# A new order of steps for a linear-attention and feed-forward kernel, with six weight casts on GpSimd

## The chip, the cores and the metric

The kernel runs on one core of one Trainium2 chip. The metric is the device time of one execution in microseconds, as the median of several runs. Three runs of the kernel before took 241.68, 242.40 and 242.57 us, a median of 242.4.

## The reference

Eight batches with eight heads, 576 rows and 64 columns go through a linear attention; its result, seen as 4608 tokens of 512, goes through a feed-forward block.

```python
def phi(x):
    return np.where(x > 0, x, np.exp(x) - 1.0) + 1.0
q_p, k_p = phi(q), phi(k)
kv = np.einsum('bhsd,bhse->bhde', k_p, v)
z = np.sum(k_p, axis=2)
num = np.einsum('bhsd,bhde->bhse', q_p, kv)
den = np.einsum('bhsd,bhd->bhs', q_p, z)[..., None] + 1e-06
x = (num / den).transpose(0, 2, 1, 3).reshape(4608, 512)
h = (x @ w1) * (x @ w2) @ w3        # w1, w2: 512 x 1024, w3: 1024 x 1024
out = h @ w_out                     # w_out: 1024 x 512
```

All inputs and the output are float32 in HBM.

## The kernel before

The kernel is one long list of steps. Every step has a short name, and `ORDER` at the top of the file is the list of these names in the order in which their instructions are issued; each engine works through its own instructions in that order. A letter at the end of a name picks the engine of the step's copy or cast (a ScalarE, v VectorE, p GpSimd), or the queue of a store.

The parts of the work and their steps:

- **Loads.** `L3.i` and `LH.i.x` load blocks of w3 (a block of 128 rows, or half of its columns), `LO.x` a slice of 256 rows of w_out, `LA.x` and `LB.x` pieces of w1 and w2, `LK.b.h`, `LQ.b.h` and `LV.b.h` four heads (half h) of a batch b of k, q and v. All are issued on SyncE's queue. They share 13 buffers, which are handed on in the order in which they come free. A weight piece is 512 KB, a half of a batch 576 KB.
- **w3 @ w_out, computed once.** `C3.i` casts a w3 block to bf16 (blocks without that step stay fp32), `CO.x` casts a w_out slice (line 217), `T3.i.x` transposes half x of a block on TensorE against an identity (four products, line 251) and copies it out of PSUM (line 252), `FW.i.x` multiplies two of the block's eight columns with the w_out slice x (two products, line 263); `FW.i.3` also casts the finished block out (line 265). `CA` and `CB` cast the pieces of w1 and w2 (lines 221 and 226).
- **Attention.** `EX` (ScalarE), `PT` and `PM` (VectorE) make phi of a half of k or q; `VC` casts v. `KV.b.h` or `KB.b` forms k_p^T v with a column of ones for z. `QP.b.h` transposes phi(q) on TensorE (nine products), `QD.b.h` by a DMA. `ND.t` makes numerator and denominator of 128 tokens and divides; `NT.t` does the products and reciprocals of three such tiles, `NM.t.i` their divisions. `XP.t` transposes a tile of x on TensorE, `XD.c.m` two tiles by a DMA.
- **Feed-forward.** Tokens are taken in nine chunks of 512. `F.c.f` is one of eight column blocks f of chunk c: four products with w1 (a), four with w2 (b), a copy of a on ScalarE, and the product a*b on VectorE. For the first chunk f 0 to 3 are split: `FI.0.f.side` is one side, `FP.0.f.side.g` one side for half of the tokens. `O.t` multiplies a tile with w3 @ w_out (eight products) and copies it out; `S.t` stores it with two DMAs, and `Q.35` is the last tile, in pieces.
- **Start.** `I.0` clears a zero tile on VectorE, `I.1` builds the fp32 identity and its bf16 copy on GpSimd, `I.2` sets the ones beside v. `H.n.i` issues n fp32 products of zeros on TensorE whose result nobody reads; there are five in all (three in `H.3.0`), and the profile counts each as two.

PSUM is handed out as four tiles for products of 512 columns (`mm`) and two larger ones (`at`), again in the order in which they come free; `T3`, `QP`, `KV` and `ND` take `at`.

The cast of a w_out slice, and the step that builds the identity, read:

```python
    def s_CO(x, e):
        copy_of(e)(out=wo_sb[:, 2 * x:2 * x + 2].rearrange("p c n -> p (c n)"), in_=raw["wo", x])
        give("ld", ("wo", x))
    ...
        elif i == 1:
            make_identity(nc, ident32)
            nc.gpsimd.tensor_copy(out=ident, in_=ident32)
```

Of the kernel before, what the change touches and what calls it, by code (L numbers as in the profile page):

```python
# [18 lines left out]


ORDER = """
I.0 H.3.0 L3.2 LO.0 I.1 T3.2.0.a H.1.1 CO.0.v FW.2.0.a T3.2.1.a H.1.2 LO.1 CO.1.a L3.4 T3.4.0.v
T3.4.1.v L3.3 T3.3.0.a LO.2 FW.4.0.v FW.4.1.a LO.3 L3.5 T3.3.1.v C3.5.a CO.2.v FW.2.1.a FW.2.2.a
CO.3.v FW.2.3.v L3.6 C3.6.v FW.3.0.a FW.3.1.v LK.0.0 T3.5.0.v LH.0.0 T3.5.1.v LQ.0.0 FW.4.2.v
EX.k.0.0 PT.k.0.0 FW.4.3.a EX.q.0.0 T3.6.0.v PM.k.0.0 FW.5.0.v FW.5.1.v L3.1 T3.6.1.a PT.q.0.0
PM.q.0.0 L3.7 FW.5.2.v FW.6.0.a FW.3.2.a FW.3.3.v FW.5.3.v LQ.0.1 T3.1.0.a C3.7.v T3.1.1.a FW.1.0.v
FW.1.1.a LK.0.1 PT.q.0.1 EX.q.0.1 PM.q.0.1 T3.7.0.a FW.6.1.v FW.6.2.a FW.6.3.a LV.0.0 I.2 T3.0.0.v
LV.0.1 EX.k.0.1 PT.k.0.1 T3.7.1.a LH.0.1 FW.7.0.a FW.7.1.v FW.1.2.v VC.0.0.v QP.0.0.v QP.0.1.a
FW.7.2.a KV.0.0.a PM.k.0.1 VC.0.1.v FW.7.3.v FW.1.3.a KV.0.1.v T3.0.1.a ND.0 FW.0.0.v LA.6 ND.1
FW.0.1.v CA.6.a LA.7 CA.7.a ND.2 FW.0.2.a XP.0.a XP.1.a ND.3 FW.0.3.a FP.0.0.0.0 LB.6 LQ.1.1  # L30
EX.q.1.1 LB.7 LA.3 XP.2.v XP.3.v FP.0.1.0.0 CB.7.a LA.2 FP.0.1.0.1 LB.3 PT.q.1.1 PM.q.1.1 FI.0.2.0
FI.0.3.0 CB.6.v FI.0.1.1 LB.2 CA.2.a LQ.1.0 CB.3.v FP.0.0.0.1 FI.0.0.1 FI.0.3.1 CB.2.v QP.1.1.v
CA.3.a PT.q.1.0 LK.1.0 FI.0.2.1 PT.k.1.0 EX.q.1.0 PM.q.1.0 F.0.4 EX.k.1.0 PM.k.1.0 F.0.5 LV.1.0
VC.1.0.a F.0.6 LK.1.1 EX.k.1.1 PT.k.1.1 PM.k.1.1 LV.1.1 LK.3.0 KV.1.0.a VC.1.1.a F.0.7 LQ.3.1
QP.1.0.a KV.1.1.v PT.k.3.0 EX.q.3.1 EX.k.3.0 O.0.a LQ.3.0 EX.q.3.0 PT.q.3.1 ND.4 ND.5 O.1.a XP.4.a
ND.6 ND.7 PM.k.3.0 LK.2.0 XP.5.a O.2.a PM.q.3.1 XP.6.v XP.7.v LQ.2.1 EX.k.2.0 LQ.2.0 PT.k.2.0
PM.k.2.0 PT.q.3.0 EX.q.2.0 LK.3.1 PM.q.3.0 O.3.a LV.4.1 F.1.0 LV.2.0 LK.4.1 S.0.s F.1.1 PT.q.2.1
EX.q.2.1 S.1.s PT.k.3.1 F.1.2 EX.k.3.1 PM.k.3.1 LK.2.1 PM.q.2.1 F.1.3 VC.2.0.a LV.2.1 PT.k.2.1
PT.q.2.0 PM.q.2.0 EX.k.2.1 F.1.4 LV.3.0 F.1.5 VC.2.1.a PM.k.2.1 F.1.6 LV.3.1 VC.3.0.v QD.2.1
EX.k.4.1 KB.2.a QD.2.0 VC.3.1.a ND.8 QD.3.0 F.1.7 KB.3.a NT.9 NM.9.0 NM.9.1 QD.3.1 XD.2.0 NM.9.2  # L40
XD.2.1 S.2.s LK.4.0 O.4.v O.5.v NT.12 LV.4.0 NM.12.0 O.6.v NM.12.1 O.7.v NM.12.2 LQ.4.1 PT.k.4.0
F.2.0 F.2.1 F.2.2 F.2.3 F.2.4 EX.k.4.0 PT.k.4.1 LQ.5.1 F.2.5 PM.k.4.1 F.2.6 VC.4.0.a LQ.4.0 VC.4.1.a
PM.k.4.0 F.2.7 S.3.s S.4.s LQ.5.0 LK.5.1 PT.q.5.0 EX.q.5.0 NT.15 PM.q.5.0 EX.q.4.1 NM.15.0 PT.q.4.1
PM.q.4.1 PT.q.4.0 LQ.7.1 S.5.s KB.4.a PT.k.5.1 O.8.v EX.k.5.1 S.6.s LK.5.0 EX.k.5.0 PT.k.5.0 XD.3.0
XD.3.1 O.9.a O.10.a O.11.v LV.5.1 F.3.0 PM.k.5.1 LK.6.0 F.3.1 PM.k.5.0 EX.q.4.0 NM.15.1 NM.15.2
LV.5.0 S.7.s S.8.s LK.6.1 F.3.2 S.9.s S.10.s VC.5.0.v PM.q.4.0 QD.4.0 EX.k.6.0 QD.4.1 F.3.3 F.3.4
EX.q.5.1 PT.q.5.1 PM.q.5.1 PT.k.6.1 F.3.5 F.3.6 F.3.7 QD.5.1 O.12.v NT.18 QD.5.0 NM.18.0 XD.4.0
NM.18.1 VC.5.1.a PT.k.6.0 KB.5.a XD.4.1 LQ.6.1 O.13.a O.14.v PT.q.7.1 O.15.v F.4.0 EX.q.7.1 PM.q.7.1
F.4.1 F.4.2 NM.18.2 LK.7.0 F.4.3 NT.21 EX.k.6.1 NM.21.0 NM.21.1 NM.21.2 LV.6.0 VC.6.0.v F.4.4 F.4.5
S.11.s S.12.s PT.k.7.0 LK.7.1 LQ.7.0 F.4.6 LV.6.1 VC.6.1.v S.13.s S.14.s F.4.7 PT.q.7.0 PM.k.6.1  # L50
LQ.6.0 PM.k.6.0 O.16.v EX.q.7.0 O.17.v PM.q.7.0 PT.q.6.1 LV.7.0 O.18.v XD.5.0 XD.5.1 EX.q.6.1
PM.q.6.1 LV.7.1 VC.7.0.a S.15.s EX.q.6.0 KB.6.a NT.24 O.19.v NM.24.0 PT.q.6.0 PM.q.6.0 QD.6.1 F.5.0
VC.7.1.v EX.k.7.1 PT.k.7.1 F.5.1 F.5.2 EX.k.7.0 NM.24.1 NM.24.2 QD.7.1 PM.k.7.0 F.5.3 F.5.4 QD.6.0
PM.k.7.1 F.5.5 S.16.s S.17.s NT.27 XD.6.0 NM.27.0 NM.27.1 QD.7.0 KB.7.a NM.27.2 F.5.6 XD.6.1 XD.7.0
F.5.7 S.18.s NT.30 S.19.s O.20.v S.20.s F.6.0 NM.30.0 NM.30.1 NM.30.2 F.6.1 XD.7.1 O.21.v NT.33
O.22.v NM.33.0 NM.33.1 O.23.v F.6.2 F.6.3 F.6.4 F.6.5 F.6.6 F.6.7 F.7.0 F.7.1 F.7.2 F.7.3 F.7.4
F.7.5 F.7.6 S.21.s S.22.s S.23.s XD.8.0 NM.33.2 XD.8.1 O.24.a O.25.v O.26.v O.27.v S.24.s S.25.s
S.26.s S.27.s F.7.7 F.8.0 F.8.1 F.8.2 F.8.3 F.8.4 F.8.5 F.8.6 F.8.7 O.28.a O.29.a O.30.a S.28.s
S.29.s S.30.s O.31.v S.31.s O.32.v S.32.s O.33.v S.33.s O.34.a S.34.b Q.35
"""  # L60


# [540 lines left out]
```

## Time and profile before

| | |
|---|---|
| median of three runs | 242.4 us |
| the profiled execution | 241.85 us |
| its span, first to last instruction | 240.1 us |
| TensorE busy | 230.6 us (96%) |
| VectorE busy | 158.2 us (66%) |
| ScalarE busy | 113.9 us (47%) |
| GpSimd busy | 1.3 us (1%) |
| moved by DMA | 55.79 MB |

PE is TensorE's products, PEld its weight loads, DVE VectorE, ACT ScalarE, POOL GpSimd, SP SyncE. A row of busy time by stretches gives the stretch, its length, then busy time and count of instructions of PE, PEld, DVE, ACT and POOL, the granted clock of TensorE, the share of the DMA engines and GB/s. A row of the timeline gives start, duration, engine, line, operation, what it writes and reads, shapes and a count where several are merged; in brackets stands the idle time ahead of it and what ended that. A row of the chain of waits gives start, duration, what it was. Products of TensorE are pipelined: the ends are modelled, and the last of a group shows its full latency.

### The profile page before, as it was taken

To read this page: it belongs to the slowest core of one execution; us is meant where nothing else is said; L and a number is where in the kernel's file an instruction comes from. 1 tells how busy PE (TensorE), PEld (TensorE's weight loads), DVE (VectorE), ACT (ScalarE), POOL (GpSimd) and SP (SyncE) were. 2 spreads that over 40 slices of the span, in tenths; PEclk is the share of its full clock that TensorE was granted. 3 is DMA by queue.
4 is the path that set the end of the run, shared out by engine and by line. 5 is a ranking of instruction groups with operands and counts; after the bars stand their busy time and mean duration, and the time that the engine had idled before them with its cause. 6 is when DMAs were issued, how large, how long until landed. Compare 5 with 4: busy or idle time off the path is not lost.

```text
span 240.1 us, 5470 instructions
## 1 busy us (share of the span) xinstructions
PE 230.6 (96%) x2227; PEld 115.8 (48%) x2246; DVE 158.2 (66%) x287; ACT 113.9 (47%) x166; POOL 1.3 (1%) x9
## 2 busy tenths in 40 slices
...
GB/s 245 418 376 405 387 387 390 388 391 389 397 272 155 183 362 360 319 195 317 257 111 279 381 369 211 123 202 111 137 120 83 3 0 44 163 15 0 45 155 149
DMA packets 52040, 55.79 MB, mean 232 GB/s; under 512 B 31280, under 2 KB 31536, under 8 KB 52016
## 3 DMA queue, kind: packets, MB, share of 16 engines
...
q8 instruction: 17, 0.28, 0.5%
...
## 4 chain that ended last, share of the span: by engine, by line
PE 90%; DMA 5%; DVE 1%; issue 1%; SPq 1%; ACT 0%
PE a_ps L482 26%; PE b_ps L482 26%; PE o_ps L535 24%; PE wf_ps L263 6%; DMA w<-in_moe_w_dram 3%; PE nd L398 2%; DMA qt<-phq 2%; PE w3p L251 2%; PE kbp L340 1%; PE qp L368 1%; PE xp L457 1%; PE kvp L340 1%; DVE w3t L252 1%; SPq L157 1%; DVE xt L458 0%
## 5 line engine op out<-in xcount | busy, mean ns | idle before, releaser
L482 PEld LDWEIGHTS <-w_sb 128*128 128x128 bf16 x584 | 56.4, 98 | 66.9 <-issue 0.9
L491 ACT COPY a_sb<-a_ps 128x512 f32<-128x512 f32 x72 | 42.1, 585 | 80.9 <-PE a_ps L482 79.0
L493 DVE TENSOR_TENSOR ab<-a_sb,b_ps 128x512 bf16<-128x512 f32 x72 | 49.1, 686 | 39.3 <-PE b_ps L482 37.5
L482 PE MATMUL a_ps<-xt,w_sb 128*128 128x512 bf16 (+1 forms) x296 | 74.0, 374 | 0.1
L482 PE MATMUL b_ps<-xt,w_sb 128*128 128x512 bf16 x288 | 73.8, 380 | 0.0
L535 PE MATMUL o_ps<-wf_sb,ab 128*128 128x512 bf16 (+2 forms) x290 | 63.5, 368 | 1.2 <-issue 0.6
L535 PEld LDWEIGHTS <-ab 128*128 128x128 bf16 x304 | 28.3, 98 | 31.2
L542 DVE COPY o_sb<-o_ps 128x512 f32<-128x512 f32 x23 | 15.9, 690 | 20.6 <-PE o_ps L535 19.5
L404 DVE TENSOR_TENSOR xn<-nd,r 128x512 bf16<-128x512 f32 (+2 forms) x45 | 24.3, 578 | 0.5
L273 ACT ACTIVATE eq<-q 128x1152 bf16<-128x1152 f32 x16 | 18.4, 1163 | 6.1 <-DVE phk L293 3.1
L273 ACT ACTIVATE ek<-k 128x1152 bf16<-128x1152 f32 x16 | 18.7, 1167 | 2.0 <-DMA k<-in_k_dram 1.9
L263 PE MATMUL wf_ps<-wo_sb,w3t 128*128 128x512 bf16 x59 | 15.7, 384 | 1.7 <-DVE wo_sb L217 1.0
L542 ACT COPY o_sb<-o_ps 128x512 f32<-128x512 f32 x12 | 7.0, 580 | 15.7 <-PE o_ps L535 15.7
L293 DVE TENSOR_TENSOR phq<-phq,eq 128x1152 bf16<-128x1152 bf16 x16 | 12.0, 752 | 1.4 <-ACT eq L273 0.9
L285 DVE TENSOR_SCALAR phq<-q 128x1152 bf16<-128x1152 f32 x16 | 12.1, 753 | 0.8 <-DMA q<-in_q_dram 0.8
L285 DVE TENSOR_SCALAR phk<-k 128x1152 bf16<-128x1152 f32 x16 | 12.1, 753 | 0.1
L293 DVE TENSOR_TENSOR phk<-phk,ek 128x1152 bf16<-128x1152 bf16 x16 | 12.0, 752 | 0.2
L327 ACT CAST vt<-v 128x1152 bf16<-128x1152 f32 x9 | 10.3, 1159 | 0.0
L398 PEld LDWEIGHTS <-qt 64*64 64x64 bf16 x576 | 6.3, 106 | 5.2 <-issue 3.0
L263 PEld LDWEIGHTS <-w3t 128*128 128x128 bf16 x64 | 5.6, 98 | 6.5 <-issue 1.5
L398 PE MATMUL nd<-kv,qt 64*64 64x65 bf16 x576 | 8.2, 194 | 0.5 <-DMA qt<-phq 0.5
L251 PE MATMUL w3p<-ident,w 128*128 128x128 f32 x40 | 6.9, 307 | 1.4 <-DMA w<-in_moe_w_dram 1.0
...
## 6 DMA issues: line engine op xcount, KB each, us to landing
...
wa<-in_moe_w_dram SPq DMA_DIRECT2D x4, 512.0 KB, 11.0
wb<-in_moe_w_dram SPq DMA_DIRECT2D x4, 512.0 KB, 11.0
```

The source lines that it names most:

```text
L251: nc.tensor.transpose(tp[:, c, :], blocks[:, 2 * x + c // 2, c % 2, :], idt)
L263: nc.tensor.matmul(wfs[i], w3ts[i][:, c, :], wo_sb[:, c, :], start=(c == 0), stop=(c == FC - 1))
L273: nc.scalar.activation(out=t, in_=raw[n, b, h], func=AF.Exp)
L285: (nc.gpsimd if e == "p" else nc.vector).tensor_scalar(out=by_set(n, t), in0=by_set("k", raw[n, b, h]), scalar1=0.0, scalar2=1.0, op0=ALU. ...
L293: nc.vector.tensor_tensor(out=t, in0=t, in1=by_set("k", es[n, b, h]), op=ALU.min)
L398: nc.tensor.matmul(dst[g * R:(g + 1) * R], qts[b, a // 2][rows, j, a % 2 * R:(a % 2 + 1) * R], kvs[b][rows, a // 2, a % 2, :], start=True, ...
L404: nc.vector.tensor_tensor(out=xn[:, :, a0:a1], in0=n4[:, :, :, 0:D], in1=r.unsqueeze(3).to_broadcast([P, 2, a1 - a0, D]), op=ALU.mult)
L482: nc.tensor.matmul(ops_[key][:, tiles.start * P:tiles.stop * P], w[:, w_row(kc), f * P:(f + 1) * P], xts[c0][:, tiles, kc, :], start=(kc = ...
L491: nc.scalar.copy(out=a_sbs[c0, f], in_=ops_[key])
L493: nc.vector.tensor_mul(out=abs_[c0][:, f, :], in0=a_sbs[c0, f], in1=ops_[key])
L535: nc.tensor.matmul(o_ps, abs_[c0][:, f, m * P:(m + 1) * P], wf_sb[:, f, cols], start=(f == 0), stop=(f == FC - 1))
L542: copy_of(e)(out=o_sbs[t], in_=o_ps)
```

## The change

Only the list of steps changes; no function does. All tiles, chunks and batches are computed with the same steps, but nearly every step stands elsewhere. Six casts move to GpSimd: `CO.0`, `CO.2`, `CA.6`, `CB.6`, `CB.7` and `CB.2`. `LO.0` becomes the first load. Of the two single zero products one now stands behind `T3.2.0` and the other between `FW.0.0` and `FW.3.3`; before, both stood among TensorE's first six steps. The list's first lines, before and after:

```diff
-I.0 H.3.0 L3.2 LO.0 I.1 T3.2.0.a H.1.1 CO.0.v FW.2.0.a T3.2.1.a H.1.2 LO.1 CO.1.a L3.4 T3.4.0.v
+LO.0 I.0 CO.0.p L3.2 LO.1 L3.7 L3.3 LO.2 CO.1.a I.1 H.3.0 LQ.0.0 T3.2.0.v H.1.2 LO.3 FW.2.0.v LH.0.0
+CO.2.p C3.7.a T3.7.0.a FW.7.0.v EX.q.0.0 T3.2.1.v CO.3.a T3.7.1.v FW.7.1.v LQ.0.1 T3.3.0.v PT.q.0.0
...
```

GpSimd from the program's start, before. `L217` is the cast of w_out, `masks.py` and `L138` build the identity:

```order
L598 UNCONDITIONAL_BRANCH
masks.py:197 MEMSET ident32_68 128x128
masks.py:199 ISA
masks.py:199 AFFINE_SELECT ident32_68<-ident32_68 128x128
L138 CAST ident_67<-ident32_68 128x128
L141 MEMSET vt0_74 128x36
L141 MEMSET vt1_75 128x36
```

The same place now:

```order
L598 UNCONDITIONAL_BRANCH
L217 CAST wo_sb_72<-wo_79 128x1024
masks.py:197 MEMSET ident32_68 128x128
masks.py:199 ISA
masks.py:199 AFFINE_SELECT ident32_68<-ident32_68 128x128
L138 CAST ident_67<-ident32_68 128x128
L217 CAST wo_sb_72<-wo_91 128x1024
L141 MEMSET vt0_74 128x36
L141 MEMSET vt1_75 128x36
L221 CAST w1_sb_70<-wa_257 128x2x512
L226 CAST w2_sb_71<-wb_280 128x2x512
```

The identity, which the first transposes on TensorE read, now stands behind the cast of the first w_out slice, and so behind that slice's load. Two more `L226` casts follow.

TensorE from the program's start, before. `w3_84` is block 2 of w3 and `w3_117` block 4, `warm` the zero products, `wf_ps` the product w3 @ w_out:

```order
L148 MATMUL warm_80<-zero_69 128x256 x3
L251 MATMUL w3p_94<-ident32_68,w3_84 128x128 x4
L148 MATMUL warm_100<-zero_69 128x256
L263 LDWEIGHTS w3t_93
L263 MATMUL wf_ps_103<-wo_sb_72,w3t_93 128x512
L263 LDWEIGHTS w3t_93
L263 MATMUL wf_ps_103<-wo_sb_72,w3t_93 128x512
L251 MATMUL w3p_106<-ident32_68,w3_84 128x128 x4
L148 MATMUL warm_112<-zero_69 128x256
L251 MATMUL w3p_120<-ident32_68,w3_117 128x128 x4
```

And now, where `w3_83` is block 2 and `w3b_122` the bf16 copy of block 7:

```order
L148 MATMUL warm_99<-zero_69 128x256 x3
L251 MATMUL w3p_106<-ident32_68,w3_83 128x128 x4
L148 MATMUL warm_112<-zero_69 128x256
L263 LDWEIGHTS w3t_105
L263 MATMUL wf_ps_116<-wo_sb_72,w3t_105 128x512
L263 LDWEIGHTS w3t_105
L263 MATMUL wf_ps_116<-wo_sb_72,w3t_105 128x512
L251 LDWEIGHTS w3b_122
L251 MATMUL w3p_125<-ident_67,w3b_122 128x128
```

The second half of block 2 no longer follows its first `FW`; block 7, which is cast on ScalarE first, stands ahead of it.

The steps around the second chunk's end and the third chunk's first products, in the list before:

```diff
-PT.q.2.0 PM.q.2.0 EX.k.2.1 F.1.4 LV.3.0 F.1.5 VC.2.1.a PM.k.2.1 F.1.6 LV.3.1 VC.3.0.v QD.2.1
-EX.k.4.1 KB.2.a QD.2.0 VC.3.1.a ND.8 QD.3.0 F.1.7 KB.3.a NT.9 NM.9.0 NM.9.1 QD.3.1 XD.2.0 NM.9.2
-XD.2.1 S.2.s LK.4.0 O.4.v O.5.v NT.12 LV.4.0 NM.12.0 O.6.v NM.12.1 O.7.v NM.12.2 LQ.4.1 PT.k.4.0
-F.2.0 F.2.1 F.2.2 F.2.3 F.2.4 EX.k.4.0 PT.k.4.1 LQ.5.1 F.2.5 PM.k.4.1 F.2.6 VC.4.0.a LQ.4.0 VC.4.1.a
+PT.q.3.0 PM.q.3.0 F.1.5 F.1.6 LQ.4.0 S.1.s S.2.s EX.q.3.1 PM.q.3.1 F.1.7 ND.8 KB.2.v O.4.a S.3.s
+QD.2.0 QD.2.1 NT.9 QD.3.1 NM.9.0 KB.3.a EX.q.4.0 O.5.a O.6.a NM.9.1 NM.9.2 QD.3.0 XD.2.0 NT.12 O.7.a
+XD.2.1 F.2.0 LQ.4.1 LK.5.1 F.2.1 F.2.2 F.2.3 LK.5.0 LQ.5.1 S.4.s NM.12.0 NM.12.1 NM.12.2 F.2.4 F.2.5
```

Of the loads, the first 29 carry the same data in both lists (w3, w_out, w1 and w2 whole, the first batch, and q of the second). Before, the 28th is w2's last piece and the 29th a half of q; now q's two halves are the 25th and 26th, and the 29th is w2's last piece, `LB.3`.

More of the change, by code (lines that the diff above doesn't have):

```diff
@@ L27 @@
[L27 to L38, printed above, removed]
@@ L45 @@
[L45 to L56, printed above, removed]
@@ L57 @@
-F.7.5 F.7.6 S.21.s S.22.s S.23.s XD.8.0 NM.33.2 XD.8.1 O.24.a O.25.v O.26.v O.27.v S.24.s S.25.s
-S.26.s S.27.s F.7.7 F.8.0 F.8.1 F.8.2 F.8.3 F.8.4 F.8.5 F.8.6 F.8.7 O.28.a O.29.a O.30.a S.28.s
-S.29.s S.30.s O.31.v S.31.s O.32.v S.32.s O.33.v S.33.s O.34.a S.34.b Q.35
+LO.0 I.0 CO.0.p L3.2 LO.1 L3.7 L3.3 LO.2 CO.1.a I.1 H.3.0 LQ.0.0 T3.2.0.v H.1.2 LO.3 FW.2.0.v LH.0.0
+CO.2.p C3.7.a T3.7.0.a FW.7.0.v EX.q.0.0 T3.2.1.v CO.3.a T3.7.1.v FW.7.1.v LQ.0.1 T3.3.0.v PT.q.0.0
+T3.3.1.a FW.2.1.v FW.2.2.v LH.0.1 FW.3.0.a FW.7.2.a L3.6 L3.4 I.2 LK.0.0 FW.7.3.a FW.2.3.v T3.0.0.a
@@ new lines @@
+EX.q.0.1 FW.3.1.a FW.3.2.v PT.q.0.1 T3.0.1.a PM.q.0.1 FW.0.0.v L3.1 H.1.1 FW.3.3.a FW.0.1.v LK.0.1
+T3.4.0.a FW.0.2.a LV.0.0 LV.0.1 L3.5 PM.q.0.0 LA.7 C3.6.v T3.6.0.v EX.k.0.0 LA.6 EX.k.0.1 CA.6.p
+PT.k.0.0 QP.0.0.v PM.k.0.0 FW.6.0.a LB.6 FW.6.1.a T3.4.1.v FW.4.0.v FW.0.3.v T3.1.0.a FW.4.1.a LB.7
+PT.k.0.1 FW.4.2.a T3.6.1.a FW.4.3.a LA.2 T3.1.1.a VC.0.0.v KV.0.0.a FW.1.0.v PM.k.0.1 LQ.1.0
+VC.0.1.v QP.0.1.v LQ.1.1 KV.0.1.a ND.0 ND.1 C3.5.a CA.7.a FW.6.2.v FW.1.1.a FW.6.3.a T3.5.0.v CB.6.p
+FW.1.2.v FW.1.3.a LB.2 ND.2 ND.3 CB.7.p LA.3 XP.0.a XP.1.a LB.3 FW.5.0.a FW.5.1.v T3.5.1.v PT.q.1.0
```

32 lines of the change are left out of this document (26 added, 6 removed).

## The prediction

> **What bounds the kernel now.** I read the page's busy times first, then busy time by stretches, then the timeline of the first 24 us, and last the chain of waits.
>
> ```profile
> span 240.1 us, 5470 instructions
> PE 230.6 (96%) x2227; PEld 115.8 (48%) x2246; DVE 158.2 (66%) x287; ACT 113.9 (47%) x166; POOL 1.3 (1%) x9
> 0.00:8.00 8.00, 6.54 (x20) 4.21 (x20) 0.97 (x2) 2.47 (x4) 1.35 (x9) 1.00 0.75 288
> 8.76:42.69 33.93, 31.66 (x333) 19.00 (x339) 26.64 (x49) 21.84 (x31) 0.00 (x0) 1.00 1.04 392
> 42.69:60.16 17.47, 17.26 (x225) 9.00 (x226) 15.91 (x33) 16.12 (x21) 0.00 (x0) 1.00 1.05 389
> 60.16:84.48 24.32, 23.64 (x351) 11.70 (x352) 21.34 (x40) 13.64 (x21) 0.00 (x0) 1.00 1.03 253
> 84.48:236.70 152.22, 151.46 (x1302) 71.87 (x1310) 93.10 (x164) 59.10 (x91) 0.00 (x0) 1.00 0.66 173
> ```
>
> The stretches run from the first products that wait for a load (8.76) to F.0.4 (42.69), to F.1.0 (60.16), to F.2.0 (84.48), to the end of PE's work. PE is idle for 0.8 of the last 152 us: nothing worth a verdict can be won there. But "busy" counts pipelined products up to their modelled ends and hides short waits, so for the early stretches I add up what their products need when nothing waits.
>
> ```profile
> 18.03 0.39 PE L251 MATMUL w3p<-ident,w3b 128*128 128x128 bf16 x4
> 18.25 2.32 PE L263 MATMUL wf_ps<-wo_sb,w3t 128*128 128x512 bf16 x10
> 26.44 1.17 PE L368 MATMUL qp<-ident,phq 128*128 128x128 bf16 x18
> 29.46 0.48 PE L340 MATMUL kvp<-vt,phk 64*64 64x65 bf16 x36
> 30.55 0.32 PE L398 MATMUL nd<-kv,qt 64*64 64x65 bf16 x16
> 32.82 0.73 PE L457 MATMUL xp<-ident,xn 128*128 128x128 bf16 x8
> 42.85 0.86 PE a_ps L482 x4
> ```
>
> Ten products of 512 columns in 2.32 us, the last taking 0.38: (2.32-0.38)/9 = 0.216 each, so an FW step (two) is 0.43 and one side of an F step (four) 0.86. Less their tails, half a bf16 block of w3 is 0.22 (18.03 to 18.25), a QP 0.5, a KV 0.4, an ND 0.25, an XP 0.28. Half an fp32 block I put at 0.5 (eight in 1.21, below).
>
> From 8.76 to 42.69 before: 31 FW 13.3, eight fp32 halves 4.0, six bf16 halves 1.3, three QP 1.5, two KV 0.8, four ND 1.0, four XP 1.1, both sides of f 0 to 3 6.9: 29.9. So 33.93-29.9 = 4.0 us are waits. From 42.69 to 60.16: four F steps 6.9, QP.1.0 0.5, two KV 0.8, four O (eight products, 1.73 each) 6.9, ND 1.0, XP 1.1: 17.2, waits 0.3. The rest of the head's loss lies before 8.76.
>
> **The change, part by part. The start.**
>
> ```profile
> 0.73 0.20 POOL masks.py:197 MEMSET ident<- 128x128 f32 x1 [0.29 <-POOLq L587]
> 1.18 2.93 PE L148 MATMUL warm<-zero 128*128 128x256 f32 x6 [1.18 <-DVE zero L135]
> 1.36 0.29 POOL L138 CAST ident<-ident 128x128 bf16<-128x128 f32 x1
> 4.19 1.10 PE L251 MATMUL w3p<-ident,w 128*128 128x128 f32 x4
> 5.08 1.06 PE L148 MATMUL warm<-zero 128*128 128x256 f32 x2
> 5.34 0.69 DVE L217 CAST wo_sb<-wo 128x1024 bf16<-128x1024 f32 x1 [4.22 <-DMA wo<-in_moe_w_out_dram]
> 6.09 0.81 PE L263 MATMUL wf_ps<-wo_sb,w3t 128*128 128x512 bf16 x2
> 6.73 0.63 PE L251 MATMUL w3p<-ident,w 128*128 128x128 f32 x4
> 7.20 0.60 PE L148 MATMUL warm<-zero 128*128 128x256 f32 x2
> 7.40 0.58 ACT L252 CAST w3t<-w3p 128x512 bf16<-128x512 f32 x1 [1.48 <-PE w3p L251]
> 7.88 1.05 ACT L217 CAST wo_sb<-wo 128x1024 bf16<-128x1024 f32 x1
> 8.76 1.21 PE L251 MATMUL w3p<-ident,w 128*128 128x128 f32 x8 [0.97 <-DMA w<-in_moe_w_dram]
> ```
>
> The first load lands at 4.2, the second at 5.3 (the cast of w_out starts then), the fourth at 8.7. In the new order POOL's first work is CO.0, the cast of w_out's slice, and the identity is built behind it. POOL's cast of 128x1024 is not in this trace. The same cast takes 0.69 on DVE and 1.05 on ACT; POOL's own cast of 128x128 takes 0.29, eight times that is 2.3. I take 1.6, between ACT's and the eightfold, and keep 0.7 to 2.3. Then ident32 is ready at 4.2+1.6+0.6 (memset to cast took 0.73 to 1.36) = 6.4 and T3.2.0 starts there, not at 4.19: 2.2 later. FW.2.0 follows at about 8.3 (6.09 before). Then T3.7.0 waits for the fourth load and ACT's cast: 8.7+1.05 = 9.8. This gate hides the whole spread of POOL's first cast: even 2.3 us end FW.2.0 before 9.8. What PE did in the old order by 9.8 and has not done now (T3.2.1, T3.4.0, T3.4.1) is in the sum that follows.
>
> **9.8 to F.0.4.** Work in the new order: 31 FW 13.3, nine fp32 halves 4.5, six bf16 halves 1.3, one zero product 0.4, four QP (QP.1.0 now lies ahead of F.0.4) 2.0, KV 0.8, ND 1.0, XP 1.1, f 0 to 3 6.9: 31.3, so 41.1 without a wait. Waits that I can place: FW.7.0 stands right behind T3.7.0 and waits for ACT's copy, 0.7 (0.58 and two hand-overs); T3.6.0 behind a DVE cast of w3, 0.3; KV.0.0 behind the cast of V, 0.6; KV.0.1 and ND.0, 0.7; the first 512-wide product behind XP.3's copy, 0.2. Together 2.5: F.0.4 at 43.6. Even would be 42.69+0.5 (for QP.1.0) = 43.2. That is +0.4.
>
> Can it be less? The loads set a floor:
>
> ```profile
> 13.76 1.05 ACT L237 CAST w3b<-w 128x1024 bf16<-128x1024 f32 x1 [2.12 <-DMA w<-in_moe_w_dram]
> 42.13 0.69 DVE L226 CAST w_sb<-wb 128x1024 bf16<-128x1024 f32 x1
> 42.78 1.16 ACT L273 ACTIVATE eq<-q 128x1152 bf16<-128x1152 f32 x1 [1.32 <-DMA q<-in_q_dram]
> ```
>
> The eighth load was waited for until 13.76, the 29th until 42.78; at 392 GB/s a load of 512 KB is 1.35 us, and the landings named here are counted from these two. In both orders the first 29 loads carry the same data, but now the 29th is w2's last piece. Its cast (DVE, 0.69) ends at 43.3, so b of F.0.4 starts no earlier and F.0.4 itself, 0.86 ahead, not before 42.4. Floor: -0.8. Upwards each wait of the list can double: +2.5.
>
> The other five POOL casts: CO.2's slice lands as the sixth load (11.0) and is needed by FW.2.2 near 14: hidden up to 3 us. CA.6, CB.6 and CB.7 land at 31.2, 32.6 and 33.9 (21st to 23rd) and run one behind another; at 1.6 each they end at 32.8, 34.4, 36.0, while f 1 starts at 34.4 (ND's chain sets that) and the first b, FI.0.3.1, stands near 39.7: hidden. CB.2 lands at 39.8, needed at 43.3: hidden. DVE loses five casts of 0.69 and ACT one of 1.05; neither sets the end there, so I count nothing.
>
> **The clock.** The profile's granted clock says 1.00 all along, but the same zero products took 2.93/6 = 0.49 each from 1.18, 1.06 for two at 5.08 and 0.60 for two at 7.20: PE doubles its rate near 6.6, after 5.4 us with hardly a pause. The new order pauses from 4.1 to 6.4 and from about 9 to 9.8, and runs dense only from 11. Bounds: nothing, or 5.4 us from 11 on at half rate, 2.7 lost, of which the later waits for loads take back some 0.6: +2.1. A slower clock cannot gain. I take +0.4 (a switch near 12.5: 0.8 lost, half of it covered).
>
> **F.1 and the first trios.**
>
> ```profile
> 60.16 0.88 PE a_ps L482 x4
> 72.18 0.78 PE L340 MATMUL kbp<-vt,phk 64*64 64x65 bf16 x72
> 75.47 0.70 PE L398 MATMUL nd<-kv,qt 64*64 64x65 bf16 x48
> 75.48 5.01 DMA qt<-phq
> 80.53 0.38 PE L398 MATMUL nd<-kv,qt 64*64 64x65 bf16 x23 [0.47 <-DMA qt<-phq]
> 84.48 0.86 PE a_ps L482 x4
> xt<-xn SPq DMA_TRANSPOSE x14, 3.3
> ```
>
> From 60.16 to 84.48 the need is eight F 13.8, ND.8 0.25, two KB (72 small products each) 1.5, NT.9 and NT.12 1.1, four O 6.9: 23.5; waits 0.8, of which 0.47 are NT.12's for a transposed q. There NT.12 stands at 80.5, two O behind NT.9; now KB.2, O.4, NT.9, KB.3, O.5 and O.6 go ahead of it and S.1 to S.3 ahead of the transposes on SP's queue. All those stores have their data by F.1.0, so they delay nothing. NT.12 comes at about 60.5+13.8+0.25+1.5+0.55+3x1.73 = 81.8, 1.3 later than the transposes needed. That wait goes. What is late next is XD.2.1: NT.9 now stands nearer to F.2.0, which leaves 7 us for normalising and a transposing DMA (3.3 in the median). I take -0.6 of the 0.8 and keep 0 to -0.8.
>
> **The rest** had under 1 us of waits; 0, with -0.3 to +0.8. The last O steps and stores are the same.
>
> Sum: +0.4+0.4-0.6+0 = +0.2 on the profiled execution (241.85 with 1.75 around the span), which lies 0.55 under the median of 242.4: 242.05+0.55 = 242.6.
>
> **The rivals.** *The clock stays low* (slower). Place: 11 to 16.5; price: 2.1 instead of 0.4, 242.6+1.7 = 244.3. It decides when the rate doubles later than about 14. For it: old PE had no pause over 0.1 us before 6.1, new PE has 2. Against: it runs 2.9 us before the first pause. [...]
>
> *POOL's casts are much longer under DVE's work* (slower). DVE works on SBUF operands beside them, and no row shows both at once. CA.6, CB.6 and CB.7 in a row may last (39.7-31.2)/3 = 2.8 each; at 4 us FI.0.3.1 starts at 43.2, 3.5 later: 246.1. Against: even the eightfold row is 2.3. [...]
>
> *Dense head* (faster): the waits of 2.5 shrink to what the load floor leaves: -0.8 instead of +0.4+0.4, hence 242.6-1.6 = 241.0. For it: ND.0 depends on V's second half, the 18th load in both orders, and seventeen FW steps stand ready as filling. Against: the start is 2 us behind.
>
> **How the numbers follow.** Forecast 242.6: 0.36. Late clock 244.3: 0.25. Long casts 246.1: 0.12. Dense head 241.0: 0.27. A difference of 0.5%, 1.2 us, is about what a measurement can tell from none: faster 0.27, same 0.36, slower 0.37. The range starts at 240.7, the dense head with 0.3 of the rest's gain, and ends at 245.0, past the late clock by the rest's 0.8; what is left out is most of the long casts and a little at either end. The forecast's own range is 241.3 to 243.7.
>
> **What would show it.** T3.2.0 near 6.4 and T3.7.0 near 9.8; zero products and FW steps at half or full rate between 10 and 17; POOL casts of 1 to 2.3 us; F.0.4 at 43.6; F.1.0 at 60.5; no wait of NT.12; F.2.0 near 84.3. The forecast is wrong if F.0.4 lies beyond 45 or before 42.8, or if XD.2.1 or any later trio stops PE for over a microsecond.

## The result and the profile after

The changed kernel took 244.51 us in the median (243.87 to 246.69, 7 runs) against 242.46 for the kernel before beside it (241.66 to 242.94, 7 runs): a ratio of 1.0106, interval 1.0068 to 1.0143. It is slower by 2.05 us. The forecast was 242.6, no change; the range, 240.7 to 245.0, holds the time, the sign was missed. Measured a second time (e13 below) the ratio was 1.0075 (1.0036 to 1.0114). The profiled execution of the kernel after took 245.19 us, 0.68 above its median, that of e13 244.48.

The page of the kernel after, then its busy time by stretches (columns as before; the second fence runs from T3.7.0 to F.0.4, F.1.0, F.2.0 and the end of TensorE's work, by the chain of waits):

```profile
span 243.4 us, 5463 instructions
PE 231.4 (95%) x2226; PEld 117.3 (48%) x2246; DVE 148.1 (61%) x276; ACT 119.5 (49%) x171; POOL 7.5 (3%) x15
```

```profile
10.60:45.29 34.69, 33.07 (x348) 21.88 (x354) 22.77 (x42) 23.90 (x35) 5.56 (x7) 1.00 1.04 391
45.29:62.09 16.80, 16.59 (x216) 8.42 (x216) 14.57 (x32) 14.35 (x19) 0.00 (x0) 1.00 1.02 363
62.09:86.85 24.76, 23.64 (x351) 11.63 (x352) 18.66 (x37) 15.61 (x23) 0.00 (x0) 1.00 0.95 214
86.85:239.70 152.85, 151.92 (x1300) 71.98 (x1309) 90.64 (x165) 62.29 (x93) 0.00 (x0) 1.00 0.68 176
```

VectorE lost 10 us of work and nothing came of it; F.1.0 and F.2.0 stand 1.9 and 2.4 us later than 60.16 and 84.48, and the end 3.3 later. The timeline from the start:

```profile
1.19 2.93 PE L148 MATMUL warm<-zero 128*128 128x256 f32 x6 [1.19 <-DVE zero L135]
4.23 1.04 POOL L217 CAST wo_sb<-wo 128x1024 bf16<-128x1024 f32 x1 [3.79 <-DMA wo<-in_moe_w_out_dram]
5.83 1.13 PE L251 MATMUL w3p<-ident,w 128*128 128x128 f32 x4 [1.71 <-POOL ident masks.py:199]
6.75 1.06 PE L148 MATMUL warm<-zero 128*128 128x256 f32 x2
9.50 1.04 ACT L237 CAST w3b<-w 128x1024 bf16<-128x1024 f32 x1 [0.23 <-DMA w<-in_moe_w_dram]
10.60 0.61 PE L251 MATMUL w3p<-ident,w3b 128*128 128x128 bf16 x4 [1.83 <-ACT w3b L237]
11.89 1.03 PE L263 MATMUL wf_ps<-wo_sb,w3t 128*128 128x512 bf16 x2 [0.68 <-ACT w3t L252]
13.99 1.06 PE L263 MATMUL wf_ps<-wo_sb,w3t 128*128 128x512 bf16 x2
14.85 1.34 PE L251 MATMUL w3p<-ident,w 128*128 128x128 f32 x8
```

GpSimd's cast lasts 1.04. The identity is ready at 5.8, and T3.7.0 waits 1.83 for ScalarE's cast of the fourth load. Two FW products still take 1.06 at 13.99 and eight fp32 products 1.34 from 14.85 (1.11 at the full rate, in e17): the full rate comes near 15. The granted clock of the page says 1.00 all the while. Further on, the timeline at the first triple tiles:

```profile
78.97 0.79 PE L340 MATMUL kbp<-vt,phk 64*64 64x65 bf16 x68
80.72 0.22 PE L340 MATMUL kbp<-vt,phk 64*64 64x65 bf16 x4 [0.97 <-issue]
118.98 1.16 ACT L327 CAST vt<-v 128x1152 bf16<-128x1152 f32 x1 [1.34 <-DMA v<-in_v_dram]
120.67 1.02 PE L482 MATMUL a_ps<-xt,w_sb 128*128 128x512 bf16 x4 [0.40 <-ACT a_sb L491]
```

NT.12 waits for nothing any more, as foretold, but KB.3 stops for 0.97 us four products ahead of its end, released by nothing that the profile shows. Behind it ScalarE stands 1.34 us waiting for v (LV.4.1, behind three stores on SyncE's queue), its copy of a comes late, and TensorE waits 0.40.

One execution of a list differs from the next, by up to 1.4 us in a stretch, so two single ones say little. The table puts together all executions whose steps stand unchanged in the stretch, the runs below included, read at the first product of F.1.0 and F.2.0 in the timeline (0.16 ahead of the chain's rows); mean, range and count. The repaired list is that of e11, e17, e18 and e19.

| stretch, us | before's list | after's list | after's, repaired |
|---|---|---|---|
| to F.1.0 | 60.7 (59.99 to 61.37, 3) | 61.7 (61.49 to 61.93, 3) | 60.9 (60.09 to 61.79, 4) |
| F.1.0 to F.2.0 | 24.1 (23.67 to 24.32, 3) | 24.6 (24.08 to 24.85, 8) | 23.9 (23.83 to 24.01, 4) |
| F.2.0 to the end | 155.7 (155.56 to 155.98, 4) | 156.9 (156.41 to 157.71, 9) | 156.3 (156.26 to 156.49, 4) |

The loss lies in all three: about 1.0, 0.5 and 1.2, together 2.7 for 1.8 to 2.1 in the medians.

### The profile page after: what moved, and what is told of

The parts are those of the page before. It is cut to its first block, busy times and chain, and to the rows that moved or that the text cites. A ratio compares the mean times of both kernels' runs of the same rounds, so it can differ in the third digit from the quotient of the medians.

```text
span 243.4 us, 5463 instructions
## 1 busy us (share of the span) xinstructions
PE 231.4 (95%) x2226; PEld 117.3 (48%) x2246; DVE 148.1 (61%) x276; ACT 119.5 (49%) x171; POOL 7.5 (3%) x15
## 4 chain that ended last, share of the span: by engine, by line
PE 85%; DMA 6%; SPq 3%; issue 2%; DVE 1%; ACT 1%; ACTq 0%; DVEq 0%
PE o_ps L535 23%; PE a_ps L482 23%; PE b_ps L482 23%; PE wf_ps L263 6%; DMA v<-in_v_dram 3%; DMA w<-in_moe_w_dram 3%; PE w3p L251 3%; PE nd L398 3%; PE kbp L340 2%; SPq L548 1%; SPq L157 1%; PE qp L368 1%; PE xp L457 1%; PE kvp L340 1%; ACT w3b L237 0%
## 5 line engine op out<-in xcount | busy, mean ns | idle before, releaser
L493 DVE TENSOR_TENSOR ab<-a_sb,b_ps 128x512 bf16<-128x512 f32 x72 | 48.6, 684 | 43.8 <-PE b_ps L482 42.2
L535 PE MATMUL o_ps<-wf_sb,ab 128*128 128x512 bf16 (+2 forms) x289 | 64.6, 367 | 0.9 <-issue 0.2
L542 ACT COPY o_sb<-o_ps 128x512 f32<-128x512 f32 x22 | 12.9, 586 | 39.5 <-PE o_ps L535 39.5
L263 PE MATMUL wf_ps<-wo_sb,w3t 128*128 128x512 bf16 x59 | 17.2, 404 | 1.1 <-ACT w3t L252 0.7
L542 DVE COPY o_sb<-o_ps 128x512 f32<-128x512 f32 x13 | 9.0, 690 | 13.7 <-PE o_ps L535 12.6
L327 ACT CAST vt<-v 128x1152 bf16<-128x1152 f32 x10 | 11.4, 1161 | 1.3 <-DMA v<-in_v_dram 1.3
L252 DVE CAST w3t<-w3p 128x512 bf16<-128x512 f32 x4 | 2.8, 689 | 12.9 <-PE w3p L251 12.9
L251 PEld LDWEIGHTS w3p<-ident,w 128*128 128x128 f32 x40 | 6.7, 208 | 4.2 <-POOL ident masks.py:199 2.4
```

What stands on the lines that cost most here:

```text
L251: nc.tensor.transpose(tp[:, c, :], blocks[:, 2 * x + c // 2, c % 2, :], idt)
L263: nc.tensor.matmul(wfs[i], w3ts[i][:, c, :], wo_sb[:, c, :], start=(c == 0), stop=(c == FC - 1))
L493: nc.vector.tensor_mul(out=abs_[c0][:, f, :], in0=a_sbs[c0, f], in1=ops_[key])
L535: nc.tensor.matmul(o_ps, abs_[c0][:, f, m * P:(m + 1) * P], wf_sb[:, f, cols], start=(f == 0), stop=(f == FC - 1))
L542: copy_of(e)(out=o_sbs[t], in_=o_ps)
```

## The experiments

**The clock.** e1 adds zero products where TensorE paused; e9 only those ahead of T3.2.0; e2 takes all five out of the kernel before.

```diff
 e1: -H.3.0  +H.5.0 ;  FW.2.0.v +H.4.3 ;  T3.7.0.a +H.1.4
 e9: -H.3.0  +H.5.0
 e2 (list before): -H.3.0  -H.1.1  -H.1.2
```

> The changed order with seven more zero products in the early pauses (H.5.0 in place of H.3.0, H.4.3 behind FW.2.0, H.1.4 behind T3.7.0). Theory 1, the clock: TensorE then hardly pauses from 1.2 to 10, its rate doubles before 8 us instead of near 15, F.0.4 comes at 44.0 to 44.4 instead of 45.3, the time falls by 1.0 to 1.5 us to about 243.2, and the spread of the runs (243.9 to 246.7) narrows. Theory 2, the order: TensorE waits for block 7's load, cast and copy whatever its rate; F.0.4 within 0.3 us of 45.3 and the time within 0.4 us of the changed kernel's.

> The kernel before without its five zero products, whose results nobody reads. Theory 1, the clock: TensorE starts at 4.2 and runs with pauses; the rate doubles only after 9 us, and the time rises by 0.5 to 1.5 us. Theory 2, the order: the early stretch waits for loads anyway; within 0.3 us of before.

> The changed order with H.5.0 in place of H.3.0: two more zero products fill the first pause (4.1 to 5.8) and nothing fills the second (8.7 to 10.6). If the rate is granted once and stays, it is full from about 7 on, also behind the second pause, and F.0.4 comes as in e1_fill (44.6). If a pause of 2 us takes it away, as one look at e3_ident suggests, T3.2.0's products run at full rate and those from 10.6 to about 14 at half, and F.0.4 stays at 45.0 or later.

e1: 244.26 us, ratio 1.0063 (1.0035 to 1.0091). e2: 243.38, 1.0004 (0.9976 to 1.0033). e9, one run: 245.29. In e1 the timeline has the full rate from 6 on, and F.0.4 still at 44.65, F.1.0 at 61.46, no earlier than in e13 (44.69 and 61.49), which has it for good only from near 14:

```profile
7.25 0.61 PE L263 MATMUL wf_ps<-wo_sb,w3t 128*128 128x512 bf16 x2 [0.35 <-DVE w3t L252]
11.82 0.63 PE L251 MATMUL w3p<-ident,w 128*128 128x128 f32 x4
```

In e2 the first transposes run at half rate until 14 (two FW products 0.59 at 14.58), F.0.4 comes 2 us later than in the profile before, and the measured ratio is that of no change. In e9 the full rate comes near 6, is still there right behind a pause of 2.4, goes near 12 and is back near 15:

```profile
6.44 0.60 PE L148 MATMUL warm<-zero 128*128 128x256 f32 x2
10.41 0.40 PE L251 MATMUL w3p<-ident,w3b 128*128 128x128 bf16 x4 [2.42 <-ACT w3b L237]
11.49 0.60 PE L263 MATMUL wf_ps<-wo_sb,w3t 128*128 128x512 bf16 x2 [0.68 <-ACT w3t L252]
11.93 0.95 PE L251 MATMUL w3p<-ident,w 128*128 128x128 f32 x4
13.10 1.06 PE L263 MATMUL wf_ps<-wo_sb,w3t 128*128 128x512 bf16 x2
```

So the late rate is there, and filling the pauses cures it (e1, from 6 on); that it costs time is not shown by any of the three. Nor is its moment fixed by the list: the kernel after has the full rate only from near 15 in its profile, but from 6 to near 7.5 and then from near 14 in e13, which is the same kernel. Each trace shows the rate of one execution, not that of the others in the median.

**The identity and the first steps.** e3 builds the identity ahead of GpSimd's first cast; e5 puts the second half of block 2 and its FW ahead of block 7, whose load they need not wait for.

```diff
 e3: I.0 +I.1 CO.0.p ... -I.1 H.3.0
 e5: FW.2.0.v +T3.2.1.v +FW.2.1.v LH.0.0 CO.2.p C3.7.a T3.7.0.a FW.7.0.v EX.q.0.0 -T3.2.1.v ... -FW.2.1.v
```

> The changed order with the identity built ahead of CO.0's cast on GpSimd. T3.2.0 then starts with its load, at 5.4 instead of 5.8. By the prediction's step that the fourth load and ScalarE's cast gate T3.7.0, that product stays at 10.6 and the time within 0.4 us of the changed kernel's. If the late identity is what costs (rival), the time falls by 0.5 us or more.

> The changed order with two ready steps, T3.2.1 and FW.2.1, moved ahead of block 7's wait (directly behind FW.2.0), nothing else. They fill part of the pause from 8.7 to 10.6, so both theories gain: by the order theory F.0.4 comes 0.9 to 1.3 us earlier than 45.1 (their 0.93 us of work, or twice that while the rate is halved, leave the dense stretch) and the time falls by 0.8 to 1.3 us against the changed kernel; by the clock theory alone (pauses matter, not what stands in them) the rate may also stay up once granted, and F.0.4 falls under 44.0. If the head's loss is set by w2's last piece instead, nothing moves.

e3: 245.55, 1.0111 (1.0072 to 1.0149): T3.2.0 starts at 5.60 instead of 5.83, then waiting for its load, and T3.7.0 waits 1.77 all the same. The gate hides the identity, as the prediction said. e5: 244.54, 1.0097 (1.0064 to 1.0131), four runs. T3.7.0's wait is gone, F.1.0 comes at 60.90 (61.7 in the mean of after's list); the time does not show it. Nor is the gain the two steps' alone: in this execution the full rate came near 10 (four bf16 products 0.42 at 10.39, 0.61 at 10.60 in the kernel after). The gain ends in a new wait, at QP.1.1 just ahead of F.0.4. VectorE, GpSimd and TensorE in e5's timeline:

```profile
40.20 1.60 DVE L285 TENSOR_SCALAR phq<-q 128x1152 bf16<-128x1152 f32 x1
40.14 1.05 POOL L226 CAST w_sb<-wb 128x1024 bf16<-128x1024 f32 x1 [4.63 <-DMA wb<-in_moe_w_dram]
42.72 0.68 PE L368 MATMUL qp<-ident,phq 128*128 128x128 bf16 x9 [0.57 <-DVE phq L293]
```

The same VectorE instruction takes 0.75 where no cast of GpSimd runs. Here it starts 0.06 behind the cast and ends 0.61 after it, as if it did its 0.75 only once the cast was nearly over.

**The casts on GpSimd.** e6 gives the six casts to GpSimd in the list before; e7 gives them back to their old engines in the list after.

```diff
 e6 (list before): -CO.0.v +CO.0.p ; -CO.2.v +CO.2.p ; -CA.6.a +CA.6.p ; -CB.6.v +CB.6.p ; -CB.7.a +CB.7.p ; -CB.2.v +CB.2.p
 e7 (list after): the same six the other way round
```

> The order before, with the same six casts on GpSimd and every step where it was. By the prediction's step that these casts are hidden and neither VectorE nor ScalarE sets the end: within 0.4 us of before; GpSimd's casts last 1.0 to 1.1. If casts on GpSimd hold up VectorE's work on SBUF (rival): F.0.4 later than 43.2 and the time up by 0.5 us or more.

> The changed order with the six casts on the engines they had before (VectorE for CO.0, CO.2, CB.6 and CB.2, ScalarE for CA.6 and CB.7). The identity is then built at once. If GpSimd's casts cost nothing: same as e3_ident, 0.9% to 1.2% over before, or slower by up to 1 us more where ScalarE's extra 2 us delay its copies. If they are what costs: within 0.5% of before.

e6: 242.25, 1.0000 (0.9978 to 1.0023). The casts alone change nothing in the time, though they and VectorE hold each other up, two casts 2.55 instead of 2.08 and phi 1.53 instead of 0.75:

```profile
36.34 2.55 POOL L226 CAST w_sb<-wb 128x1024 bf16<-128x1024 f32 x2 [4.67 <-DMA wb<-in_moe_w_dram]
36.46 1.53 DVE L285 TENSOR_SCALAR phq<-q 128x1152 bf16<-128x1152 f32 x1
```

e7: 253.05, 1.0441 (1.0411 to 1.0471), far beyond what was expected. Its waits have one line for it:

```profile
PE w3p L251 <- ACT w3t L252: 6.3, 1, 6.3
```

Most of it is one cast, CA.6: ScalarE waits for its load, and the copy for which TensorE waits stands behind it.

```profile
31.84 1.04 ACT L221 CAST w_sb<-wa 128x1024 bf16<-128x1024 f32 x1 [7.32 <-DMA wa<-in_moe_w_dram]
32.79 0.58 ACT L252 CAST w3t<-w3p 128x512 bf16<-128x512 f32 x1
33.43 1.12 PE L251 MATMUL w3p<-ident,w 128*128 128x128 f32 x4 [6.35 <-ACT w3t L252]
```

A cast that stands early in the list and waits for its load, here 7.32 us, blocks the copies behind it on ScalarE; on GpSimd only the identity, the ones beside v and other casts are queued. The new order needs CA.6 there; the five others were not moved back singly.

**Head against tail.** e4 takes the list before up to F.1.0 and the remaining steps in after's order.

```diff
 e4: list before up to F.1.0, then what is left in the order of the list after
```

> The order before up to F.1.0, then what is left in the changed order. If the whole loss lies in the first 60 us (theories 1 and 2 together): F.1.0 at 60.2, F.2.0 at 84.3 or earlier, time 241.8 to 242.5. If the changed order also loses behind F.1.0 (theory 3, seen in its trace as waits at KB.3 and of ScalarE for v: 0.4 us to F.2.0 and 0.9 us behind it): F.1.0 at 60.2, time 243.2 to 243.8.

249.57, 1.0274 (1.0222 to 1.0325): 6.5 us go between F.1.0 and F.2.0, in waits of the seam itself (3.2 for a copy of a; the loads that the steps behind need are issued too late for them). It tells nothing of head and tail; only its stretch behind F.2.0, 156.2, could be read.

**KB.3 and NT.12.** e10 puts eight long products between NT.9 and KB.3. e12 moves NT.12 one O step back in the list before.

```diff
 e10: NM.9.0 -KB.3.a EX.q.4.0 O.5.a +KB.3.a O.6.a
 e12 (list before): O.5.v -NT.12 LV.4.0 -NM.12.0 O.6.v +NT.12 +NM.12.0 -NM.12.1 O.7.v +NM.12.1
```

> The changed order with KB.3 moved behind O.5, nothing else. In the changed kernel TensorE stops for 0.97 us four products before KB.3's end with nothing that it waits for, after some 400 short instructions in 6 us (KB.2, NT.9, KB.3). If that is TensorE's own instruction stream running dry (theory 3), long products between NT.9 and KB.3 end it: no such wait, F.1.0 to F.2.0 in 23.9 instead of 24.8 us, time lower by up to 1 us. If KB.3 waits for data (rival), the wait moves with it and F.2.0 stays.

> The order before with NT.12 and its divisions moved behind O.6, nothing else. The wait of 0.47 us for the transposed q, which the prediction counted as the gain of this stretch, then goes: F.1.0 to F.2.0 in 23.8 to 23.9 instead of 24.3 us and the time lower by 0.3 to 0.5 us, ratio 0.998 to 0.999. If XD.2's transposes for F.2.0 are just behind it, nothing is gained.

e10: 244.70, 1.0090 (1.0060 to 1.0120); the stop is gone and F.1.0 to F.2.0 takes 24.00, as expected. Its time against e13's on that chip (244.56) doesn't show these 0.8 us. e12: 242.54, 0.9978 (0.9952 to 1.0004); the wait for the transposed q is gone and the stretch takes 23.69 instead of 24.32. But e2, which leaves this stretch as it was, has no such wait either and takes 23.67, and in e6 the wait is 0.34: the gain that the prediction credited is there in some executions of the kernel before and not in others.

The stop's place and its end say more. In e9 8 instructions more stand ahead of it on TensorE, in e1 28 (two and seven zero products, each two products and two weight loads). A product of KB.3 comes with a weight load (72 of phk for its 72 products in the kernel after), and the stop lies 4 and 14 products earlier, which is 8 and 28 instructions: 68 products of KB.3 stand ahead of it in the kernel after, 64 in e9, 54 in e1, and none is cut off in e10:

```profile
80.48 0.26 PE L340 MATMUL kbp<-vt,phk 64*64 64x65 bf16 x8 [0.55 <-issue]
79.46 0.35 PE L340 MATMUL kbp<-vt,phk 64*64 64x65 bf16 x18 [0.20 <-issue]
80.52 0.78 PE L340 MATMUL kbp<-vt,phk 64*64 64x65 bf16 x72
```

So the stop belongs to a place in TensorE's instructions, not to a step or its data. The page has a DMA queue for instructions, with 17 transfers of 16 KB:

```profile
q8 instruction: 17, 0.28, 0.5%
```

In all nine executions that have the stop, a transfer of this queue ends shortly ahead, and TensorE goes on 1.3 to 1.5 us behind its end (in the kernel after 79.22 and 80.72, in e1 77.99 and 79.46). TensorE waiting for its next instructions fits all of this. That the queue is TensorE's is inferred (it alone has 4472 of the 5463 instructions), and no run changes the loading itself.

**After once more, and all repairs.** e13 is the kernel after, unchanged. e11 puts the repairs together: the identity first, zero products in the pauses, T3.2.1 and FW.2.1 early, KB.3 behind O.5, and the two v loads that ScalarE waited for exchanged. e14, e15 and e16 then took the wait at QP.1.1 in the wrong way, by moving QP.1.1 behind F.0.4: alone, with the repairs of the order, and with zero products too.

```diff
 e11: +I.1 -I.1 ; -H.3.0 +H.4.0 ; FW.2.0.v +T3.2.1.v +H.2.3 +FW.2.1.v ; T3.7.0.a +H.1.4 ; -H.1.1 ; O.5.a +KB.3.a ; LV.4.1 <-> LV.5.1
 e14: -QP.1.1.a FI.0.0.1 F.0.4 +QP.1.1.a
 e15: e14 and T3.2.1, FW.2.1, KB.3, LV.4.1, LV.5.1 as in e11
 e16: e15 and -H.3.0 +H.5.0 ; FW.2.1.v +H.2.3 ; T3.7.0.a +H.1.4
```

> The changed kernel once more, as it is, beside the repaired ones on one chip: 1.007 to 1.014 of before. If its rate doubles at another time in this execution (theory 1: the pauses leave that to chance), F.0.4 moves by about half of that time and the wait at KB.3 stays between 0.8 and 1.1 us.

> The changed order with all repairs together: identity first on GpSimd, T3.2.1 and FW.2.1 ahead of block 7, zero products only in the pauses that are left (four at the start, one each behind T3.2.0 and T3.7.0, two behind T3.2.1), KB.3 behind O.5, and the load for VC.4.1 exchanged with the later needed LV.5.1. If theories 1 to 3 name the whole loss: full rate from 7 us on, F.0.4 at 43.3 to 43.8, F.2.0 at 84.0 to 84.8, and 242.2 to 243.0 us, within 0.3% of before. If the rest of the order carries a loss of its own: 243.3 us or more.

> The kernel after with QP.1.1 behind F.0.4 instead of ahead of it, nothing else. In three of the runs so far (the early T3.2.1, the fill, the repetition of after) TensorE stood 0.57, 0.57 and 0.31 us at QP.1.1, because VectorE's phi of that half took 1.60 and 1.34 us instead of 0.75 while GpSimd's cast of w2 ran. Theory that this wait is a term of the loss: F.0.4 comes 0.5 us earlier by the step that is moved and up to 0.57 more by the wait that F.0.4 now covers, F.1.0 comes 0.3 to 0.6 us earlier than the 61.65 of the repetition, and the time is 0.1 to 0.2% better than the kernel after. Rival, that something else on the way to F.1.0 is as late (ScalarE's copy of the transposed half, or the KV step behind it): F.1.0 stays within 0.1 us.

> The kernel after with T3.2.1 and FW.2.1 directly behind FW.2.0, QP.1.1 behind F.0.4, KB.3 behind O.5, and LV.4.1 and LV.5.1 exchanged: all order repairs together, no zero product added. If order alone made the loss, F.1.0 comes at about 60.5 (61.06 of the early T3.2.1 less 0.57), F.2.0 at 84.5 and the median at 242.5 to 243.1, like the kernel before within 0.2%. If the late clock has a price of its own of about 1 us, the median stays at 243.5 or above and the next run, which adds the zero products, is about 1 us faster.

> The same with five zero products in H.5.0 in place of H.3.0, two behind FW.2.1 and one behind T3.7.0, so that TensorE's full rate is granted near 6 and kept. If the late clock has a price of its own: about 1 us faster than the run without them. If it has none in this order, because the stages behind wait for loads and casts anyway: within 0.3 us of that run, or slower by up to the 0.25 us that an added zero product can cost each.

e13: 244.56, 1.0075 (1.0036 to 1.0114). e11: 243.57, 1.0030 (1.0007 to 1.0053). e14: 246.57, 1.0173 (1.0138 to 1.0207), against its expectation: F.0.4 comes earlier, 44.27, but from there to F.1.0 it takes 18.80 instead of 16.80, of which QP.1.1 itself is 0.5. F.0.4's second side now waits for the cast of w2 on VectorE, and the KV steps behind for the cast of v:

```profile
46.08 0.82 PE L482 MATMUL b_ps<-xt,w_sb 128*128 128x512 bf16 x3 [0.56 <-DVE w_sb L226]
51.20 0.48 PE L340 MATMUL kvp<-vt,phk 64*64 64x65 bf16 x36 [0.35 <-ACT vt L327]
```

QP.1.1 had been the cover for that cast; VectorE's queue, not the one transpose, was late. e15: 244.28, 1.0088 (1.0060 to 1.0116); e16: 244.60, 1.0097 (1.0067 to 1.0127). F.0.4 comes 0.26 earlier with zero products, the time does not. As a test of the late clock the pair fails, since e15 had the full rate near 10 without them (four bf16 products 0.43 at 10.01).

**What holds VectorE up.** e17 is e11 with the cast CB.2 on ScalarE, which stood idle there; e19 is e11 unchanged, on the same chip; e18 has the order's repairs and that cast, but zero products and identity as in the kernel after.

```diff
 e17: e11 and -CB.2.p +CB.2.a
 e18 (list after): FW.2.0.v +T3.2.1.v +FW.2.1.v ; O.5.a +KB.3.a ; LV.4.1 <-> LV.5.1 ; -CB.2.p +CB.2.a
 e19: e11
```

> The earlier run with all repairs, with one more: the cast of w2's piece 2 goes from GpSimd to ScalarE, at the same place in the list. There ScalarE stands 0.4 to 0.6 us idle twice, and the piece is read only by F.0.4's b side. Theory that VectorE is held up by GpSimd's cast: PT.q.1.1 and PM.q.1.1 take 0.75 us each (one of them took 1.40), the wait of 0.37 at QP.1.1 goes, F.0.4 and F.1.0 come 0.3 to 0.5 us earlier. Rival, that VectorE's long row is that piece of code's own: it stays at 1.3 to 1.6 and nothing moves.

> The kernel after with T3.2.1 and FW.2.1 directly behind FW.2.0, KB.3 behind O.5, LV.4.1 and LV.5.1 exchanged and the cast of w2's piece 2 on ScalarE; the zero products and the identity stay as in the kernel after. F.0.4 comes 0.57 us earlier than in the early T3.2.1 run (43.7 by the chain of waits), F.1.0 at about 60.5, F.2.0 at 84.4. If the late clock has no price of its own, its time is within 0.3 us of the run with all repairs and ScalarE's cast; if it has one of about 1 us, it is that much slower.

> The earlier run with all repairs, unchanged, beside the two others on the same chip: 1.003 again within 0.25%. What the two others gain or lose is read against it.

e17: 242.31, 0.9985 (0.9965 to 1.0004). e18: 242.70, 0.9997 (0.9975 to 1.0018). e19: 242.97, 1.0002 (0.9980 to 1.0024). VectorE in e17 and then in e19, and what TensorE does with it in e19:

```profile
40.14 0.75 DVE L285 TENSOR_SCALAR phq<-q 128x1152 bf16<-128x1152 f32 x1
41.00 0.76 DVE L293 TENSOR_TENSOR phq<-phq,eq 128x1152 bf16<-128x1152 bf16 x1
```

```profile
40.80 1.28 POOL L226 CAST w_sb<-wb 128x1024 bf16<-128x1024 f32 x1 [4.56 <-DMA wb<-in_moe_w_dram]
41.09 1.59 DVE L285 TENSOR_SCALAR phq<-q 128x1152 bf16<-128x1152 f32 x1
43.61 0.68 PE L368 MATMUL qp<-ident,phq 128*128 128x128 bf16 x9 [0.57 <-DVE phq L293]
```

With GpSimd's last cast gone both phi rows take 0.75 and TensorE does not wait at QP.1.1: that stretch of VectorE's is GpSimd's doing. F.1.0 stands at 60.09 in e17, 61.79 in e19; of these 1.7 us the wait explains 0.57, and a wait for the cast of v at KV.0 (1.31 in e19, 0.36 in e17) 0.95. The medians lie 0.66 apart and the intervals overlap, so the cast's price is not shown in the time. Nor is there a wait at QP.1.1 in the profile after itself, where GpSimd's cast had ended (41.24) when VectorE began (41.30). And e11 and e19 are one kernel, slower by 0.3% on one chip and even on another: these ratios do not settle differences of that size.

e18 is the answer to the case. It leaves the zero products and the late identity as in the kernel after. In its profiled execution (242.54) the full rate is there from 6 and gone before 8, and then it is half until 14:

```profile
6.43 0.60 PE L148 MATMUL warm<-zero 128*128 128x256 f32 x2
7.94 1.06 PE L251 MATMUL w3p<-ident,w 128*128 128x128 f32 x4
13.13 1.06 PE L263 MATMUL wf_ps<-wo_sb,w3t 128*128 128x512 bf16 x2
13.99 1.34 PE L251 MATMUL w3p<-ident,w 128*128 128x128 f32 x8
```

And yet it is as fast as the kernel before. On the same chip e5, which has only the first two of its moves, was at 1.0097. So what the kernel after lost, it lost by the places of five steps and the engine of one cast, taken together: F.1.0 comes 1.0 earlier than in the mean of after's list, the trios take 0.8 less, the rest 0.6. What each of the six is worth in the medians was not shown.

## Why the prediction was right or wrong

**The start: right, T3.7.0's gate included.** Predicted T3.2.0 at 6.4 and T3.7.0 at 9.8. Measured 5.83 and, in four executions, 10.60, 9.66, 9.74 and (identity first) 9.56. The cast took 1.04 where 1.6 was taken. The gate hid it (e3).

**9.8 to F.0.4: the sum about right, the parts not.** Predicted F.0.4 at 43.6, or 44.0 with the clock's 0.4, which the list of signs leaves out; measured 45.13 and 44.69, once beyond the 45 that it named as a sign of being wrong. But 42.69, from which the forecast counts, was the earliest of three executions of that list (43.46 in e4, 44.06 in e12), and by the table the loss ahead of F.1.0 is 1.0, against 0.8 in the sum. Of the waits that could be placed, FW.7.0's was there with 0.68 and ND.0's with 0.43. Two things were missing. T3.2.1 and FW.2.1 stood ready behind the gate that hid the identity, and I had put them into "the sum that follows" instead of asking who stood idle meanwhile: in e5 F.1.0 comes 0.8 earlier, in part by the rate. And the list of waits ended at the first 512-wide product; that QP.1.1, just ahead of F.0.4, hangs on VectorE's queue was not seen (0.31 in e13, 0.57 in e1 and e5, none in the profile after). The load floor of 42.4 for F.0.4 counted the last cast from its load, not from its place on VectorE.

**The five other GpSimd casts: their side effect was missed, with "I count nothing".** Each is hidden as a cast and lasts 1.04. What they cost is VectorE's time beside them, up to 0.85 for an instruction. The rival of long casts had looked for the loss in casts of 4 us; the runs show it more in VectorE's instructions: a tensor_scalar of 0.75 took 1.60, a tensor_tensor of 0.76 took 1.21 to 1.40, always beside a cast, and casts of 1.04 took up to 1.42. It costs nothing in the list before (e6, 1.0000); in the list after TensorE's wait at QP.1.1 shows it in some executions, and the medians of e17 and e19 do not tell its price from none.

**The clock: the premise wrong, the size not contradicted.** The term was +0.4 with a switch near 12.5, an estimate between two bounds; the switch came near 15 (near 14 in e13), so the rival that gave 244.3 had its premise and almost the measured time. But the rival's price of 2.1 was not there, and that its 244.3 lay near the measured time was luck: e18, with the late rate, takes 242.70, and e17, with the full rate from 6 (and the identity first), 242.31; without any zero product e2 is at 1.0004, and e1, which fills the pauses, 0.3 under e13. These differences are 0.1 to 0.4, none of them clear of zero, so the forecast's +0.4 may stand, by luck too, as its switch was too early. What takes the rest back can be seen in e17: it waits 0.72 for a cast of w_out at 15.47, 0.31 for a load of w3 at 19.89 and 0.36 for the cast of v at 28.46, and e18 has none of these waits. I had put that at 0.6 of 2.7 us; as far as these two show, it was most of it.

**F.1 and the first trios: the sign failed.** This is one of the two steps that failed. Predicted -0.6, measured +0.5 by the table. The wait named did go; the 24.32 from which it was counted was the longest of three executions of that list, and e2, without the wait, takes 23.67. What came instead was on none of my lists of what is late next: TensorE stopping by itself, 0.97 us in KB.3, when ND.8, KB.2, NT.9 and KB.3 stood almost side by side, with one O step among them; it is 0.9 to 1.05 in six executions of that stretch, 0.55 in e9 and 0.20 in e1. With O.5 between NT.9 and KB.3 the stretch takes 23.8 to 24.0 in all seven executions that have it, as the kernel before does without its wait.

**The rest: the term that was most mis-sized, and the other step that failed.** Predicted 0, at most +0.8, in one sentence that argued from the list before having no waits there. Measured +1.2 by the table. ScalarE's wait for v, which the exchange of two loads takes away, makes 0.5 to 0.6 of that in the mean; from execution to execution TensorE's wait behind it goes from none that the profile lists (e13) to 1.32 (e3). Of the remaining 0.6 only a part can be pointed at: with the same 288 short products of KB behind F.2.0, TensorE was busy with them for 3.7 us in e18 and 3.4 before. The rest of it stays open; no wait in e18's trace shows it.

By the table the misses are 0.2 ahead of F.1.0 (1.0 instead of 0.8), 1.1 at the trios and 1.2 behind: 2.5 in all, of which the medians show 1.6 to 1.9. That the time still fell into the range is owed to the late clock's rival, which set its upper end and whose price did not come. A forecast of no change stood on a gain that only some executions have to give and on places that had been looked at for their present waits instead of their new neighbours.
